# Strassen projection of a fused gMLP block: its operand sums moved from GpSimd to VectorE, with five VectorE operations moved earlier and the last pair's closing piece moved later

## The chip, the cores and the metric

The kernel runs on one core of a Trainium2 chip. The metric is the device time of one execution in microseconds (us). Three runs of the kernel before took 311.89, 312.03 and 312.06 us, so the median is 312.03 us. The profile is of one execution; it records a span of 309.7 us, and some 2.3 us of the device time lie around that span.

The engines are named as in the profile: PE (TensorE), PEld (its weight loads), DVE (VectorE), ACT (ScalarE), POOL (GpSimd), and SP (SyncE, which here only issues DMAs). SPq and DVEq are the engines' sequencers.

## What is computed

```python
h = layernorm(x) * (1 + ca) + sa                      # x: 2048 x 640
x = x + ga * A(h, k, v, shift_k, ssm_k, ssm_D)        # a long convolution
h = layernorm(x) * (1 + cb) + sb
z = gelu(h @ w_in)                                    # 2048 x 1728
z1, z2 = z[:, :864], layernorm(z[:, 864:])
g = w_sp @ z2 + b_sp[:, None]                         # w_sp: 2048 x 2048
out = x + gb * ((z1 * g) @ w_out)                     # w_out: 864 x 640
```

`u = z1 * g` below. The change lies in the last two lines, and in the order of some preparations during the two lines ahead of them.

## The kernel before

The rows are cut into 16 tiles of 128. After the long convolution (to some 147 us of the span) comes the **z stage**: layernorm, modulation, the product with `w_in`, GELU and the second layernorm. All work up to the first pair of the mix stage is recorded as operations with numbers and then written out in the order of a table by hand, `ORDER`; an entry such as `D1047` puts operation 1047 on DVE at that place. Each engine works through its own instructions in the order in which they stand.

**The mix stage** takes the tiles in pairs: pair p is tile p and tile p + 8, with p = 0 to 7. Pair 0 is in the table; pairs 1 to 7 are the loop at the end of the kernel. `w_sp @ z2` is computed for a pair by Strassen's method in Winograd's form, with seven products instead of eight (`product(p, m)`, each of 8 matmuls 128x432). They come in the order 1, 5, 2, 6, 7, 3, 4 and share four PSUM banks: products 2, 3 and 4 accumulate onto a bank that an earlier product has filled.

- The weights' operand sums are `s_sum(p, k)`, DVE, 128x1024, line 987. They are made one pair ahead.
- After product 2 DVE runs `c11` (L1029); after product 6 `partial` (L1034); after product 7 `c22` (L1038, L1039, L1040). Product 4 accumulates onto the bank that L1038 reads, so PE may not start it before L1038 has ended.
- After products 3 and 4 come `last_sum` (L1045, L1046, twice) and `turn_u` (L1051), a transposing DMA on SP that makes `uT`, the transposed u of a tile.

**The projection** `u @ w_out` of a pair is Strassen-Winograd as well (`project_pair`). The 864 features make 7 chunks; six of them form two halves of three chunks, the seventh (96 rows) is added plainly. Its operand sums are

- `V[0..3]` and `V5`, sums of `w_out` (already multiplied by `gb`, L1076), 128x960 each and one of 96x320, made once (L1160, L1234);
- `R[0..3]`, sums of the pair's `uT` chunks, 128x384 each, made for each pair by `u_sums` (L1170).

`project_pair` returns four pieces that the loop places. `begin` and `most` hold most of its matmuls, on four more banks called a, d, b and c_; ACT copies two of them (L1196, L1198), POOL adds rows of x to them (L1199, L1204, L1205, L1206), DVE makes L1203 and L1211. `sums` is L1216, L1217 and an output DMA (L1218). `end` is the piece that reuses bank c_ after L1216 has read it: 4 matmuls (`V[3]`, `V5`), L1223 and an output DMA (L1224).

In the loop before, the iteration of pair p runs products 1, 5, 2, then `end` of pair p - 2, then products 6, 7, 3, 4, then `begin`, `most` and `sums` of pair p - 1, and then `u_sums(p)` on POOL. After the loop the last two tiles, 7 and 15, are projected plainly (`project`, L1139, L1141), with `end` of pair 6 between them.

Of the kernel before, what the change touches and what calls it, by code (L numbers as in the profile page):

```python
# [10 lines left out]
ALU = mybir.AluOpType  # L11
# [65 lines left out]
D859 A865 P886 A881 A883 G909 P853 D1053 D1049 D966 G907 D968 P884 A854 D862 D807 P892 G908 D800 P871 A885 D810 S910  # L77
D803 A887 A872 D912 P890 D863 D876 P888 G911 P878 A913 D873 A891 A915 D914 A889 A879 P916 A893 G970 S1041 P923 D797
P940 D1054 D971 A972 A917 G975 D811 D974 D804 A941 P926 D869 D855 P919 A927 D866 P952 A920 D852 P933 P954 D856 S1040
D870 D1055 D1052 A953 A924 D1058 D918 P937 G973 D1059 S976 D978 G828 P930 A979 A934 D1050 D928 A938 G977 D980 D925 A981  # L80
D829 A955 D942 D877 D833 D921 A931 D831 P958 G894 S1043 P982 P996 P1006 A983 D932 A959 A830 A832 D922 A1007 D935 D939
D943 D1057 D936 D895 P999 P1003 D1056 A1000 P992 D929 A1004 A997 P950 A993 A951 P948 D994 D898 D1005 A897 A896 P946
D1001 P1018 A949 P985 D998 D1062 G960 A947 D1002 D899 D1008 P989 A1019 A986 P956 D961 P1024 P1012 A964 D963 D962 D1009
A990 D987 A965 D991 P1014 D995 D984 A957 D988 A1025 A1013 G1026 A1015 D1051 P944 D1066 P1070 D1027 A945 D1063 A1030
P1020 A1029 S1042 D1064 P1072 A1071 D1028 A1021 D1031 D1065 P1074 D1068 D1067 P1077 D1075 P1081 P1022 A1073 P1076 D1069
D1078 D1082 D1079 P1083 S1080 P1010 P1016 A1017 D1084 A1011 S1085 D1047 A1023 D1061 D1046 D1048 D1060
"""


# [39 lines left out]
def kernel(  # L129
# [20 lines left out]
    nc = tc.nc  # L150
    _, S, D = A_q.shape
# [5 lines left out]
    NFT = (Fh + P - 1) // P  # L157
# [4 lines left out]
    HS = D // NH  # L162
# [47 lines left out]
    with ExitStack() as pctx:  # L210
# [17 lines left out]
        sums = consta.tile([P, NT, 2], F32)  # L228
# [6 lines left out]
        op = plan.op  # L235
# [735 lines left out]
        def load_w(t):  # L971
            wTs[t] = bwork.tile([P, NT, P], BF16, tag="wT", bufs=WB, name="wT")
            nc.sync.dma_start_transpose(wTs[t][:], B_w_sp[t * P:(t + 1) * P, :])  # L973
# [7 lines left out]
        def s_sum(p, k):  # L981
            if p not in Ss:
                Ss[p] = [bwork.tile([P, HT, P], BF16, tag="S%d" % i, bufs=2, name="S%d" % (i + 1)) for i in range(4)]
            S = Ss[p]
            x, y, o = ((a_of(p, 1, 0), a_of(p, 1, 1), ALU.add), (S[0][:], a_of(p, 0, 0), ALU.subtract),
                       (a_of(p, 0, 0), a_of(p, 1, 0), ALU.subtract), (a_of(p, 0, 1), S[1][:], ALU.subtract))[k]
            nc.vector.tensor_tensor(S[k][:], x, y, op=o)  # L987
# [13 lines left out]
        def product(p, m, alloc):  # L1001
            S = Ss.get(p)
            lhs = (a_of(p, 0, 0), a_of(p, 0, 1), S and S[3][:], a_of(p, 1, 1), S and S[0][:], S and S[1][:], S and S[2][:])[m - 1]
            rhs = (lambda s_: zb(s_, 1, 0), lambda s_: zb(HT + s_, 1, 0), lambda s_: zb(HT + s_, 1, 1),
                   lambda s_: T[4][:, s_:s_ + 1, :], lambda s_: T[1][:, s_:s_ + 1, :], lambda s_: T[2][:, s_:s_ + 1, :],
                   lambda s_: zb(s_, 1, 1))[m - 1]
            more = m in (2, 3, 4)
            if not more:
                part[p, BANK[m]] = alloc(BANK[m])
            ps = part[p, BANK[m]]  # L1010
            for s_ in range(HT):
                nc.tensor.matmul(ps[:, :FC], lhsT=lhs[:, s_, :], rhs=rhs(s_), start=(s_ == 0 and not more), stop=(s_ == HT - 1),  # L1012
                                 skip_group_check=more)
# [111 lines left out]
    w_o = T["w_o"]  # L1125
# [22 lines left out]
    fl = fsz[-1]  # L1148
    vbuf = bigp.tile([P, (4 * KT + 1) * HS], BF16, tag="big", bufs=SLOTS["big"], name="V")
    V = [vbuf[:, i * KT * HS:(i + 1) * KT * HS].rearrange("p (k d) -> p k d", d=HS) for i in range(4)]  # L1150
    V5 = vbuf[:, 4 * KT * HS:]
    rbuf = span.tile([P, 2, 4, KT, P], BF16, tag="Z", bufs=SLOTS["Z"], name="R")
    obuf = span.tile([P, 6, HS], F32, tag="Z", bufs=SLOTS["Z"], name="O")
# [4 lines left out]
    def weight_sum(e, k):  # L1158
        x, y = ((wo_b(0, 1), wo_b(0, 0)), (wo_b(1, 1), V[0]), (wo_b(1, 1), wo_b(0, 1)), (wo_b(1, 0), V[1]))[k]
        e.tensor_tensor(V[k], x, y, op=ALU.subtract)  # L1160
# [4 lines left out]
    def u_sums(p):  # L1165
        R = [rbuf[:, p % 2, i] for i in range(4)]
        lo, hi = p, p + HT
        for k, (x, y, o) in enumerate(((u_of(hi, 0), u_of(hi, 1), ALU.add), (R[0], u_of(lo, 0), ALU.subtract),
                                       (u_of(lo, 0), u_of(hi, 0), ALU.subtract), (u_of(lo, 1), R[1], ALU.subtract))):
            nc.gpsimd.tensor_tensor(R[k], x, y, op=o)  # L1170
        return R

    def rows(i):
# [6 lines left out]
    def project_pair(p, R):  # L1180
        lo, hi = p, p + HT
        U = {(i, j): (lambda k, t=t, j=j: uTs[t][:, j * KT + k, :]) for i, t in ((0, lo), (1, hi)) for j in range(2)}
        B = {(i, j): (lambda k, i=i, j=j: w_o[:, i * KT + k, j * HS:(j + 1) * HS]) for i in range(2) for j in range(2)}
        S_ = [lambda k, i=i: R[i][:, k, :] for i in range(4)]
        V_ = [lambda k, i=i: V[i][:, k, :] for i in range(4)]

        def rest(t, j):
            return (lambda k: uTs[t][:fl, NFT - 1, :]), (lambda k: w_o[:fl, NFT - 1, j * HS:(j + 1) * HS]), 1
        ot = [bwork.tile([P, D], BF16, tag="ot", bufs=3, name="ot") for _ in range(2)]
        x_of = lambda i, j: xt[:, (lo, hi)[i], j * HS:(j + 1) * HS]  # L1190
        m1, m5, s, s12, s21, s22 = (rows(i) for i in range(6))
        a, d, b, c_ = (obank() for _ in range(4))

        def begin():
            piece(a, U[0, 0], B[0, 0], KT, True, True)
            nc.scalar.copy(m1, a[:, :HS])  # L1196
            piece(d, S_[0], V_[0], KT, True, True)
            nc.scalar.copy(m5, d[:, :HS])  # L1198
            nc.gpsimd.tensor_tensor(m5, m5, x_of(1, 1), op=ALU.add)  # L1199

        def most():
            piece(b, S_[1], V_[1], KT, True, True)
            nc.vector.tensor_tensor(s, b[:, :HS], m1, op=ALU.add)  # L1203
            nc.gpsimd.tensor_tensor(s22, s, m5, op=ALU.add)  # L1204
            nc.gpsimd.tensor_tensor(s12, s, x_of(0, 1), op=ALU.add)  # L1205
            nc.gpsimd.tensor_tensor(s21, s, x_of(1, 0), op=ALU.add)  # L1206
            piece(c_, S_[2], V_[2], KT, True, False)
            piece(c_, *rest(hi, 1), False, True)
            piece(a, U[0, 1], B[1, 0], KT, False, False)
            piece(a, *rest(lo, 0), False, True)  # L1210
            nc.vector.tensor_tensor(ot[0][:, 0:HS], a[:, :HS], x_of(0, 0), op=ALU.add)  # L1211
            piece(d, S_[3], B[1, 1], KT, False, False)
            piece(d, *rest(lo, 1), False, True)

        def sums():
            nc.vector.tensor_tensor(ot[1][:, HS:D], c_[:, :HS], s22, op=ALU.add)  # L1216
            nc.vector.tensor_tensor(ot[0][:, HS:D], d[:, :HS], s12, op=ALU.add)  # L1217
            nc.sync.dma_start(out_nat[:, lo, :], ot[0][:])  # L1218

        def end():  # L1220
            piece(c_, U[1, 1], V_[3], KT, False, False)
            piece(c_, lambda k: uTs[hi][:fl, NFT - 1, :], lambda k: V5[:fl, :], 1, False, True)
            nc.vector.tensor_tensor(ot[1][:, 0:HS], c_[:, :HS], s21, op=ALU.add)  # L1223
            nc.sync.dma_start(out_nat[:, hi, :], ot[1][:])  # L1224
        return begin, most, sums, end

    load_w(3)
    load_w(3 + HT)
    weight_sum(nc.gpsimd, 2)
    weight_sum(nc.vector, 0)  # L1230
    R = u_sums(0)
    weight_sum(nc.gpsimd, 1)
    weight_sum(nc.gpsimd, 3)
    nc.gpsimd.tensor_tensor(V5[:fl, :], w_o[:fl, NFT - 1, 0:HS], w_o[:fl, NFT - 1, HS:D], op=ALU.subtract)  # L1234
    end = None
    for p in range(1, HT):
        nxt = p + 1 < HT
        product(p, 1, bank)
        keep(p, 1)
        product(p, 5, bank)  # L1240
        keep(p, 5)
        if nxt:
            s_sum(p + 1, 0)
            s_sum(p + 1, 1)
        product(p, 2, bank)
        c11(p)
        if nxt:
            s_sum(p + 1, 2)
        if end:
            end()  # L1250
        product(p, 6, bank)
        partial(p)
        product(p, 7, bank)
        c22(p)
        begin, most, sums, end = project_pair(p - 1, R)
        product(p, 3, bank)
        last_sum(p, "d", 0, 1)
        turn_u(p, 0)
        product(p, 4, bank)
        last_sum(p, "c", 1, 0)  # L1260
        turn_u(p, 1)
        if p + 3 < HT:
            load_w(p + 3)
            load_w(p + 3 + HT)
        begin()
        most()
        if nxt:
            s_sum(p + 1, 3)
        sums()
        if nxt:  # L1270
            R = u_sums(p)
    project(HT - 1)
    end()
    project(NT - 1)
# [30 lines left out]
```

## Time and profile before

| | us |
|---|---|
| device time, median of 3 runs | 312.03 (311.89 to 312.06) |
| span of the profiled execution | 309.7 |
| busy in the span: PE, DVE, POOL, ACT | 295.1, 272.4, 186.2, 164.1 |
| products of pair 0 end, pair 1 of the loop starts on PE | 203.6 |
| last matmul of the program ends | 306.9 |

How to read the rows: a timeline row gives start, duration, engine, line, operation, what it writes and reads, and how many instructions it stands for; in brackets at its end stands how long the engine was idle just before, and what ended that. Durations are from issue to completion, so instructions that follow each other on DVE overlap in the records by 0.05 to 0.1 us, and a row of matmuls includes 0.16 us of the pipeline's tail, during which the next matmul may already run. POOL's spans are rough.

### The profile page before, as it was taken

The numbers are of one execution on the slowest core, as the hardware profiler recorded it, in microseconds if no ns is written. First come the engines' busy times: TensorE is split into PE (matmuls) and PEld (weight loads), VectorE is DVE, ScalarE is ACT, GpSimd is POOL, SyncE is SP. The second block draws the span as 40 slices with busy tenths as digits, with TensorE's granted clock in tenths as the row PEclk, the third lists the DMA queues.
The fourth block names the chain that finished last, engine by engine and source line by source line (L and its number), as shares of the span: only waits on it lengthen the run. The fifth ranks groups of instructions, "written<-read, shape, count | busy, mean of one in ns | idle before, by whom it ended". The sixth has DMA issues, their size and how long they took to land.

```text
span 309.7 us, 6534 instructions
## 1 busy us (share of the span) xinstructions
PE 295.1 (95%) x2485; PEld 195.4 (63%) x2485; DVE 272.4 (88%) x532; ACT 164.1 (53%) x298; POOL 186.2 (60%) x209
## 2 busy tenths in 40 slices
PE   6979999999999999899999999998899999999995
PEld 1357678797889998755554555555455656565554
DVE  7797999999999999998859788999999878888574
ACT  4799699989787864466647799031111111021110
POOL 5724955856869999695705312049658474573922
PEclk9799999999999999999999999999999999999999
DMA  7999999999674949505898800073387593730323
GB/s 176 224 251 200 243 299 199 249 254 207 170 158 115 184 110 273 211 3 108 191 181 180 150 1 1 2 145 51 73 167 150 132 194 73 168 80 21 83 55 110
DMA packets 127954, 45.23 MB, mean 146 GB/s; under 512 B 117071, under 2 KB 127156, under 8 KB 127924
## 3 DMA queue, kind: packets, MB, share of 16 engines
q1 hardware_dynamic: 127770, 44.78, 65.5%
q8 instruction: 19, 0.31, 0.4%
q14 instruction: 11, 0.09, 0.1%
q10 hardware_dynamic: 154, 0.05, 0.1%
HBM read 16.11 MB, written 5.24 MB: 69 GB/s over the span
## 4 chain that ended last, share of the span: by engine, by line
PE 40%; DVE 6%; DMA 4%; SPq 4%; POOL 2%; issue 1%; ACT 0%; DVEq 0%; ACTq 0%
PE ps L1012 20%; PE po L1178 7%; PE pu L244 4%; PE pz L244 4%; DMA Z<-Z 3%; SPq L973 2%; PE pz L1012 2%; PE pu L1012 1%; DVE S L987 1%; PE po L1139 1%; SPq L1073 1%; DMA uT<-u 1%; POOL Z L844 1%; DVE V L1160 1%; POOL xt L697 1%
## 5 line engine op out<-in xcount | busy, mean ns | idle before, releaser
L244 PEld LDWEIGHTS <-Z 128*128 128x128 bf16 x320 | 31.1, 98 | 28.4 <-issue 1.2
L244 PE MATMUL pu<-X,M 128*128 128x128 bf16 (+1 forms) x480 | 45.9, 237 | 0.4 <-DVE Tf L461 0.3
L244 PEld LDWEIGHTS <-M 128*128 128x128 bf16 x480 | 37.1, 98 | 5.3 <-issue 0.6
L475 POOL TENSOR_TENSOR W<-Tf 128x256 bf16<-128x256 f32 x43 | 31.3, 745 | 12.7 <-DVE Tf L461 5.0
L1012 PEld LDWEIGHTS <-S 128*128 128x128 bf16 x256 | 25.0, 98 | 21.2
L244 PE MATMUL pu<-big,Z 128*128 128x432 bf16 x160 | 33.6, 346 | 0.5 <-ACT M L919 0.4
L244 PE MATMUL pz<-big,Z 128*128 128x432 bf16 x160 | 32.6, 346 | 0.1
L1196 ACT COPY O<-po 128x320 f32<-128x320 f32 x7 | 3.0, 427 | 55.9 <-PE po L1178 55.9
L247 ACT CAST X<-s 128x1024 bf16<-128x1024 f32 x30 | 30.7, 1024 | 3.5 <-PE s L244 3.4
L461 DVE TENSOR_TENSOR Tf<-pu,KH 128x1024 f32<-128x1024 f32 x25 | 30.0, 1214 | 1.4 <-PE pu L244 1.0
L1012 PEld LDWEIGHTS <-wT 128*128 128x128 bf16 x192 | 18.7, 98 | 17.6 <-issue 2.0
L244 PEld LDWEIGHTS <-G 128*128 128x128 bf16 x330 | 25.0, 98 | 3.3 <-issue 0.6
L247 ACT CAST KH<-pu 128x512 bf16<-128x512 f32 x40 | 23.5, 598 | 6.0 <-PE pu L244 6.0
L247 ACT CAST Z<-pz 128x512 bf16<-128x512 f32 x34 | 19.9, 599 | 8.2 <-PE pz L244 8.1
L1199 POOL TENSOR_TENSOR O<-O,xt 128x320 f32<-128x320 f32 x7 | 6.3, 906 | 28.0 <-ACT O L1198 28.0
L1012 PE MATMUL ps<-T,S 128*128 128x432 bf16 x112 | 22.7, 346 | 0.0
L1012 PE MATMUL ps<-X,wT 128*128 128x432 bf16 x112 | 22.7, 346 | 0.0
L244 PE MATMUL sm<-big,dg 128*128 128x512 bf16 (+1 forms) x80 | 21.3, 395 | 0.7 <-ACT dg L535 0.7
L1012 PE MATMUL ps<-X,S 128*128 128x432 bf16 x112 | 21.6, 346 | 0.0
L244 PEld LDWEIGHTS <-X 128*128 128x128 bf16 x288 | 18.2, 97 | 5.2 <-issue 1.4
L244 PE MATMUL s<-F1bd,X 128*128 128x256 bf16 x128 | 19.2, 273 | 0.3 <-ACT X L247 0.3
L925 DVE BATCH_NORM_STATS2 stz<-X 128x6 f32<-128x432 bf16 x32 | 17.8, 589 | 1.6 <-ACT X L919 1.6
(208 smaller groups left out, 679.9 us busy)
## 6 DMA issues: line engine op xcount, KB each, us to landing
wm<-in_w_mod_dram SPq DMA_DIRECT2D x6, 800.0 KB, 6.1
xt<-in_A_q_dram SPq DMA_DIRECT2D x4, 640.0 KB, 5.2
out_dram<-ot SPq DMA_DIRECT2D x15, 160.0 KB, 2.2
big<-in_B_w_in_dram SPq DMA_DIRECT2D x2, 1080.0 KB, 10.7
X<-in_A_ssm_k_dram SPq DMA_DIRECT2D x4, 512.0 KB, 7.0
kv_scr<-big SPq DMA_DIRECT2D x4, 512.0 KB, 3.2
X<-kv_scr SPq DMA_DIRECT2D x4, 512.0 KB, 4.5
w_o<-in_B_w_out_dram SPq DMA_DIRECT2D x6, 160.0 KB, 3.4
```

Source lines behind the costliest of these rows:

```text
L244: nc.tensor.matmul(o, lhsT=w, rhs=x, start=start, stop=stop)
L247: (e.copy if e is nc.scalar else e.tensor_copy)(dst, src)
L461: e.tensor_tensor(T_[:], (tl[pu] if src is None else tl[src])[:, :, :, None, :].to_broadcast(shape), tl[KH][:, :, None, :, :].to_broadcast ...
L475: e.tensor_tensor(tl[W][:, :, o, :], T_[:, :, 0, o, :], T_[:, :, 1, 1 - o, :], op=ALU.add if o else ALU.subtract)
L697: op("GD" if u < NU - 1 else "D", "res", lambda e: e.tensor_tensor(sl, sl, gl, op=ALU.add), r=[("gh", (u, g))], w=[("xt", (u, n)) for n in ...
L844: e.tensor_scalar(dst, xt[:, n, :], rstd2[:, n:n + 1], nmr2[:, n:n + 1], op0=ALU.mult, op1=ALU.add)
L925: op("D", "stz", lambda e, i=i, n=n, fc=fc: e.bn_stats(out=stz[:, n, fc, :], in_=tl[z2][:, i, fc * FC:(fc + 1) * FC]), r=[(z2, (i, fc))], ...
L973: nc.sync.dma_start_transpose(wTs[t][:], B_w_sp[t * P:(t + 1) * P, :])
L987: nc.vector.tensor_tensor(S[k][:], x, y, op=o)
L1012: nc.tensor.matmul(ps[:, :FC], lhsT=lhs[:, s_, :], rhs=rhs(s_), start=(s_ == 0 and not more), stop=(s_ == HT - 1), skip_group_check=more)
L1178: nc.tensor.matmul(ps[:, :HS], lhsT=w(k), rhs=x(k), start=start and k == 0, stop=stop and k == n - 1, skip_group_check=True)
L1199: nc.gpsimd.tensor_tensor(m5, m5, x_of(1, 1), op=ALU.add)
```

## The change

1. `u_sums` runs on DVE instead of POOL, and stands one iteration later: `R = u_sums(p - 1)` after product 5 of pair p and the first two `s_sum`s, ahead of product 2 and `c11`.
2. The five sums `V[0..3]` and `V5`, of which POOL made four, are all made by DVE, in one row ahead of the loop.
3. In the table, five DVE operations that stood at its end are moved up into the z stage: 1046, 1047, 1048 and 1051, four of the seven multiplications of `w_out` by `gb` (L1076), and 1061, the sum `s_sum(1, 3)` (L987).
4. In the last iteration (p = 7) `end` of pair 5 stands after product 4, instead of between products 2 and 6.

```diff
-            nc.gpsimd.tensor_tensor(R[k], x, y, op=o)
+            nc.vector.tensor_tensor(R[k], x, y, op=o)
...
-    weight_sum(nc.gpsimd, 2)
-    weight_sum(nc.vector, 0)
-    R = u_sums(0)
-    weight_sum(nc.gpsimd, 1)
-    weight_sum(nc.gpsimd, 3)
-    nc.gpsimd.tensor_tensor(V5[:fl, :], w_o[:fl, NFT - 1, 0:HS], w_o[:fl, NFT - 1, HS:D], op=ALU.subtract)
+    for k in (0, 2, 1, 3):
+        weight_sum(nc.vector, k)
+    nc.vector.tensor_tensor(V5[:fl, :], w_o[:fl, NFT - 1, 0:HS], w_o[:fl, NFT - 1, HS:D], op=ALU.subtract)
...
             s_sum(p + 1, 1)
+        R = u_sums(p - 1)
         product(p, 2, bank)
...
-        if end:
+        if end and nxt:
             end()
...
-        begin, most, sums, end = project_pair(p - 1, R)
...
+        if not nxt:
+            end()
+        begin, most, sums, end = project_pair(p - 1, R)
         begin()
         most()
...
         sums()
-        if nxt:
-            R = u_sums(p)
```

Of the table, the entries `D1047 D1046 D1048` now follow `D1059`; `D1061 D1051` follow `D929`.

**DVE, between pair 0 and the c22 of pair 1.** `w_o` is `w_out`, `S_...` the weights' sums, `u_...` the rows of u, `T_...`, `s_...` and `c_...` intermediate sums, `ps` and `po` PSUM banks. Before:

```order
L1046 TENSOR_TENSOR u_2796<-c,G_81 128x432
L1076 TENSOR_TENSOR w_o<-w_o,gb_bf 128x640
L987 TENSOR_TENSOR S_3083<-wT,S_3081 128x1024
L1076 TENSOR_TENSOR w_o<-w_o,gb_bf 128x640 x2
L987 TENSOR_TENSOR S_3082<-wT 128x1024
L1160 TENSOR_TENSOR V<-w_o 128x960
L987 TENSOR_TENSOR S_3464<-wT 128x1024
L987 TENSOR_TENSOR S_3465<-S_3464,wT 128x1024
L1029 SCALAR_TENSOR_TENSOR u_2797<-ps,bcol,M_80 128x432
```

and the same stretch now:

```order
L1046 TENSOR_TENSOR u_2796<-c,G_81 128x432
L987 TENSOR_TENSOR S_3082<-wT 128x1024
L1160 TENSOR_TENSOR V<-w_o 128x960 x2
L1160 TENSOR_TENSOR V<-w_o,V 128x960 x2
L1231 TENSOR_TENSOR V<-w_o 96x320
L987 TENSOR_TENSOR S_3460<-wT 128x1024
L987 TENSOR_TENSOR S_3461<-S_3460,wT 128x1024
L1170 TENSOR_TENSOR R<-uT 128x384
L1170 TENSOR_TENSOR R<-R,uT 128x384
L1170 TENSOR_TENSOR R<-uT 128x384
L1170 TENSOR_TENSOR R<-uT,R 128x384
L1029 SCALAR_TENSOR_TENSOR u_2797<-ps,bcol,M_80 128x432
```

Four operations have left this place for the z stage; three V sums, V5 and the four R sums of pair 0 have come in from POOL.

**DVE, where the moved operations now stand in the z stage** (`Z` is the modulated input, `X_...` z2, `mvz` and `stz` its statistics):

```order
L929 BN_AGGR mvz<-stz 128x2
L987 TENSOR_TENSOR S_3083<-wT,S_3081 128x1024
L1076 TENSOR_TENSOR w_o<-w_o,gb_bf 128x640
L925 BN_STATS stz<-X_3135 128x6
L942 TENSOR_SCALAR X_2857<-X_2857,mvz,rstdz 128x864
```

The sum and one multiplication stand between a finished statistic and a row (L925) that waits for ACT; the other three multiplications stand in the same manner ahead of an L896 that waits for a transposing DMA.

**DVE, last pair and end of the program.** Before:

```order
L1217 TENSOR_TENSOR ot<-po,O 128x320
L1029 SCALAR_TENSOR_TENSOR u_2797<-ps,bcol,G_81 128x432
L1223 TENSOR_TENSOR ot<-po,O 128x320
L1034 TENSOR_TENSOR s_4320<-ps,m_4283 128x432
L1038 TENSOR_TENSOR c_4331<-ps,s_4320 128x432
```

and, later in the same list, now:

```order
L1046 TENSOR_TENSOR u_2797<-c,G_81 128x432
L1045 SCALAR_TENSOR_TENSOR c<-ps,bcol,s_4314 128x432
L1046 TENSOR_TENSOR u_2798<-c,G_81 128x432
L1223 TENSOR_TENSOR ot<-po,O 128x320
L1203 TENSOR_TENSOR O<-po,O 128x320
L1211 TENSOR_TENSOR ot<-po,xt 128x320
```

L1223 of pair 5, which stood behind `c11` of pair 7, now stands behind the pair's last L1046. On PE its four matmuls stand behind product 4, and on SP its output DMA behind the last two `turn_u`.

More of the change, by code (lines that the diff above doesn't have):

```diff
@@ L79 @@
 P940 D1054 D971 A972 A917 G975 D811 D974 D804 A941 P926 D869 D855 P919 A927 D866 P952 A920 D852 P933 P954 D856 S1040
[L80 to L86, printed above, removed]
+D870 D1055 D1052 A953 A924 D1058 D918 P937 G973 D1059 D1047 D1046 D1048 S976 D978 G828 P930 A979 A934 D1050 D928 A938
+G977 D980 D925 A981 D829 A955 D942 D877 D833 D921 A931 D831 P958 G894 S1043 P982 P996 P1006 A983 D932 A959 A830 A832
+D922 A1007 D935 D939 D943 D1057 D936 D895 P999 P1003 D1056 A1000 P992 D929 D1061 D1051 A1004 A997 P950 A993 A951 P948
+D994 D898 D1005 A897 A896 P946 D1001 P1018 A949 P985 D998 D1062 G960 A947 D1002 D899 D1008 P989 A1019 A986 P956 D961
+P1024 P1012 A964 D963 D962 D1009 A990 D987 A965 D991 P1014 D995 D984 A957 D988 A1025 A1013 G1026 A1015 P944 D1066 P1070
+D1027 A945 D1063 A1030 P1020 A1029 S1042 D1064 P1072 A1071 D1028 A1021 D1031 D1065 P1074 D1068 D1067 P1077 D1075 P1081
+P1022 A1073 P1076 D1069 D1078 D1082 D1079 P1083 S1080 P1010 P1016 A1017 D1084 A1011 S1085 A1023 D1060
 """
```

## The prediction

> **What bounds the kernel now.** I read the page's busy shares first, then the waits of PE from 160 us on, then the busy time of each engine pair by pair in the mix stage, then the timeline around each wait of PE. The page and the waits (who waited for whom: total, times, longest):
>
> ```profile
> PE 295.1 (95%) x2485; PEld 195.4 (63%) x2485; DVE 272.4 (88%) x532; ACT 164.1 (53%) x298; POOL 186.2 (60%) x209
> ```
> ```profile
> PE ps L1012 <- DVE c L1038: 1.5, 2, 0.8
> PE po L1178 <- DVE ot L1216: 1.1, 1, 1.1
> PE po L1139 <- DMA uT<-u: 0.6, 1, 0.6
> ```
>
> PE is the bound, and in the last half of the program it stands still four times: three times for DVE, once for a transposing DMA at the end. Where those three lie is seen from the busy times of pairs 1, 2 and 6 (length of the stretch; then PE, PEld, DVE, ACT, POOL; clock, DMA share, GB/s), each stretch cut from the pair's first product to the next pair's:
>
> ```profile
> 203.60:217.63 14.03, 13.25 (x79) 7.52 (x77) 13.75 (x15) 3.35 (x7) 12.24 (x8) 1.00 0.53 100
> 217.63:233.35 15.72, 13.95 (x83) 7.89 (x81) 14.82 (x23) 1.99 (x4) 9.64 (x10) 1.00 0.61 124
> 274.26:287.89 13.63, 13.63 (x84) 7.91 (x82) 12.06 (x19) 1.99 (x4) 8.51 (x9) 1.00 0.24 58
> ```
>
> A settled pair takes 13.63 us with PE full, at full clock. Pairs 1 and 2 are longer, and in them DVE is busy nearly throughout. The timeline tells why DVE is late there:
>
> ```profile
> 205.23 2.33 POOL L1160 TENSOR_TENSOR V<-w_o 128x960 bf16<-128x960 bf16 x1 [14.78 <-PE ps L1012]
> 205.62 2.46 DVE L1160 TENSOR_TENSOR V<-w_o 128x960 bf16<-128x960 bf16 x1
> 212.75 4.32 POOL L1160 TENSOR_TENSOR V<-w_o,V 128x960 bf16<-128x960 bf16 x2
> 213.31 1.62 PE L1012 MATMUL ps<-T,wT 128*128 128x432 bf16 x8 [0.78 <-DVE c L1038]
> 213.36 1.85 DVE L1039 TENSOR_TENSOR c<-c,m 128x432 f32<-128x432 f32 x1
> 215.25 2.29 DVE L1040 TENSOR_TENSOR u<-c,G 128x432 bf16<-128x432 f32 x1
> 223.23 0.70 PE L1178 MATMUL po<-V,uT 128*128 128x320 bf16 x4 [1.05 <-DVE ot L1216]
> 229.03 1.62 PE L1012 MATMUL ps<-T,wT 128*128 128x432 bf16 x8 [0.72 <-DVE c L1038]
> 282.30 0.61 DVE L1038 TENSOR_TENSOR c<-ps,s 128x432 f32<-128x432 f32 x1 [0.53 <-PE ps L1012]
> 283.01 0.61 DVE L1039 TENSOR_TENSOR c<-c,m 128x432 f32<-128x432 f32 x1
> 283.65 0.61 DVE L1040 TENSOR_TENSOR u<-c,G 128x432 bf16<-128x432 f32 x1
> ```
>
> L1039 and L1040 take 0.61 us in pair 6, and 1.85 and 2.29 us in pair 1, beside POOL's V sums. So DVE operations that read two SBUF tensors come to a stand while POOL does the same. The one V sum on DVE shows it exactly: it starts at 205.62, POOL's ends at 207.56, and DVE's at 208.08, 0.52 later.
>
> **Part by part.** *The sums that leave POOL* (parts 1 and 2 of the change) take away this cause. What it costs now is read from the lengths of the pairs; pair 1 has no `end` piece, whose price stands in pair 7:
>
> ```profile
> 292.27 0.71 PE L1178 MATMUL po<-V,uT 128*128 128x320 bf16 x4
> 292.81 1.62 PE L1012 MATMUL ps<-T,S 128*128 128x432 bf16 x8
> ```
>
> Pair 2 is 15.72 - 13.63 = 2.09 us too long. `end` takes 292.81 - 292.27 = 0.54 us of PE; pair 1 does without it, so its length should be 13.09, and it is 0.94 too long. Together 3.03 us. The three idle times 0.78, 1.05 and 0.72 make 2.55; the difference is three times the 0.16 us of the pipeline's tail, which the row of `end` shows too (0.71 long, the next one 0.54 later).
>
> What do the sums cost on DVE? No R, and no V without POOL beside it, is in the trace. The nearest rows are other two-input bf16 operations of DVE while POOL was quiet:
>
> ```profile
> 163.76 0.64 DVE L987 TENSOR_TENSOR S<-wT 128x1024 bf16<-128x1024 bf16 x1
> 172.24 0.48 DVE L1076 TENSOR_TENSOR w_o<-w_o,gb_bf 128x640 bf16<-128x640 bf16 x1
> 188.53 1.05 DVE L997 TENSOR_TENSOR X<-X,X 128x1728 bf16<-128x1728 bf16 x1
> ```
>
> A V (960 elements) lies between 0.48 and 0.64; I take 0.61, as it is close to 1024. The 1728-element row works on four pieces of 432 and costs no more for it, so the three pieces of 320 in V add nothing. An R (384 elements) is at most 0.48; carried on from 1024 and 640 it is 0.37, from 1728 and 1024 it is 0.27. I take 0.33, four of them 1.3, with 1.1 to 1.9 as bounds; V5 at most that, 0.3.
>
> Is there room on DVE in pair 1? The last row of pair 0 ends at 203.29, and L1038 has to end by the time when product 4 may start:
>
> ```profile
> 202.68 0.61 DVE L1046 TENSOR_TENSOR u<-c,G 128x432 bf16<-128x432 f32 x1
> 207.52 1.32 POOL L1170 TENSOR_TENSOR R<-uT 128x384 bf16<-128x384 bf16 x1
> 209.44 3.08 PE L1012 MATMUL ps<-X,S 128*128 128x432 bf16 x16
> ```
>
> Products 7 and 3 end their issue at 209.44 + 3.08 - 0.16 = 212.36. From 203.29 DVE now has: one S 0.64, four V 2.44, V5 0.3, two S 1.28, four R 1.3, `c11` 0.66, an S 0.64, L1034 0.6, L1038 0.61: 8.47 us, so 211.8, 0.6 us ahead of need. In it R begins at 207.95, and `uT` of pair 0 is there by then, since POOL's R began at 207.52. With the upper prices (V 0.64, R 0.48) it is 212.5, and 0.1 us of the hole would stay. Pair 1 then leaves DVE where the settled pairs have it, and the two holes of pair 2 have no cause left. I count the whole 3.0.
>
> *The wait that this adds.* R on DVE waits for the pair's `uT`, and `c11`, an S sum, L1223, L1034 and L1038 are queued behind it; PE waits for the last. Pair 3 has the transposes that landed latest:
>
> ```profile
> 250.13 0.69 DVE L987 TENSOR_TENSOR S<-S,wT 128x1024 bf16<-128x1024 bf16 x1
> 250.55 1.03 POOL L1170 TENSOR_TENSOR R<-uT 128x384 bf16<-128x384 bf16 x1 [1.01 <-DMA uT<-u]
> 255.04 0.61 DVE L1038 TENSOR_TENSOR c<-ps,s 128x432 f32<-128x432 f32 x1 [0.79 <-PE ps L1012]
> ```
>
> They landed at 250.5, DVE is through with the S sum at 250.8: no wait. R ends at 252.1, and 0.66 + 0.64 + 0.48 + 0.6 later, at 254.5, DVE is ready for L1038, which waits for PE until 255.04 in any case. And L1038 may be later still by the time of product 3, 1.46 (half of the 2.92 above), less its own 0.61. So a settled pair hides R with 0.5 us to spare, 1.3 until PE waits. Cost 0.
>
> *The five moved operations* (part 3) are counted above as gone from pair 0's end. Where they go, DVE waits:
>
> ```profile
> 171.91 0.41 DVE L896 TENSOR_SCALAR Z<-Z,cb_col,sb_col 128x512 bf16<-128x512 bf16 x1 [1.90 <-DMA Z<-Z]
> 180.46 0.61 DVE L925 BATCH_NORM_STATS2 stz<-X 128x6 f32<-128x432 bf16 x1 [1.13 <-ACT X L919]
> ```
>
> Three multiplications, 3 x 0.48 = 1.4, stand in the gap of 1.90; the sum and the fourth, 0.64 + 0.48 = 1.12, in that of 1.13, with the overlap of the records to spare. Their inputs are there, since other L1076 and other sums of the same weights have run by then. Cost 0; if a cover were gone, a few tenths, and only if PE then waits.
>
> *The end* (part 4). Pair 7, with the rows that set the last steps:
>
> ```profile
> 293.08 0.49 DVE L1223 TENSOR_TENSOR ot<-po,O 128x320 bf16<-128x320 f32 x1
> 299.06 1.39 PE L1178 MATMUL po<-V,R 128*128 128x320 bf16 x9
> 299.92 0.61 DVE L1046 TENSOR_TENSOR u<-c,G 128x432 bf16<-128x432 f32 x1
> 299.26 2.57 SPq L1051 DMA_TRANSPOSE uT<-u  x2
> 301.38 0.30 PE L1178 MATMUL po<-w_o,uT 96*128 96x320 bf16 x1
> 302.30 2.08 PE L1139 MATMUL po<-w_o,uT 128*128 128x320 bf16 x14 [0.61 <-DMA uT<-u]
> ```
>
> Times here are those of before. With the four matmuls of `end` behind product 4, products 6, 7, 3 and 4, the last L1046 and the transposes come 0.54 earlier: the transpose is issued at 298.72 and lands at 301.7, not 302.25. PE's own work is the same in sum, so all that can be won is its idle time, 0.6 by the row, at most 0.55 by the transposes. But L1223 now runs behind the last L1046, which ends at 299.99, and so ends at 300.4. The third group of V x R matmuls writes the bank that L1223 reads; nine take 1.39 - 0.16, so it would start at 299.06 + 6 x 0.137 = 299.88, and has to wait until some 300.45. The row at 301.38 then ends its issue at 301.52 + 0.57 = 302.09, and PE comes to tile 7 there instead of at 302.30. I take 0.2; bounds 0 and 0.55. On SP the output DMA of L1224 goes out behind both transposes, at about 301.3. Its buffer is wanted again by L1141 of tile 7 at about 303.2:
>
> ```profile
> out_dram<-ot SPq DMA_DIRECT2D x15, 160.0 KB, 2.2
> ```
>
> It lands at 303.5, so L1141 may be 0.3 late, and nothing waits for that for the next microsecond.
>
> **The sum.** Against the profiled execution: 309.7 - 3.0 - 0.2 = 306.5. The median of the runs lies 2.3 above that span, and I keep the 2.3: **308.8 us**, 1.0% less. A difference of 0.2%, 0.6 us, is about what a measurement of this kernel tells from none.
>
> **The rivals.** *VectorE becomes the bound* (the other side). DVE is busy 12.06 us of a settled pair's 13.63. Four R at 0.33 add 1.3. But two S sums of pair 6 ran beside POOL's R:
>
> ```profile
> 277.39 1.28 DVE L987 TENSOR_TENSOR S<-S,wT 128x1024 bf16<-128x1024 bf16 x1
> 279.42 1.44 DVE L987 TENSOR_TENSOR S<-wT 128x1024 bf16<-128x1024 bf16 x1
> ```
>
> They fall back to 0.64, which gives the same 1.4 again. That speaks against. For it speaks that R has no row on DVE. Without any relief 1.57 us are free, so R binds from 0.39 each on, with the relief from 0.75; at POOL's 1.03 four R are 4.1, DVE needs 12.06 - 1.4 + 4.1 = 14.8, and six pairs (2 to 7) lose 1.15 each, 6.9 us, against 3.2 won: 315.7. It is slower than before from R = 0.88 on. The Trainium skill, Perfetto Trace Analysis, section Optimizing Scalar/DVE Operations, speaks against this change in the same sense: work is to be taken off VectorE where it is saturated, if need be to GpSimd, though it adds that between those two this may not help, since they share a port. The rule's first half would give this rival, its second half my forecast; the V rows above agree with the second. Chance 0.04.
>
> *V is slow by itself.* The only V on DVE took 2.46 us. If that is its own price and not POOL's doing, four take 9.8 instead of 2.44, L1038 of pair 1 ends at 219.2, PE waits 6.8 us there instead of 0.94, and 2.3 are won elsewhere: 315.6. Against it: 1728 elements took 1.05. It is slower than before from about 1.6 us per V on. The Trainium skill, SBUF — State Buffer, section Who interferes with whom, says that an operation of VectorE with two SBUF inputs and one of GpSimd that reads SBUF exclude each other for a whole instruction, so that the later one stands still; by that V is the 0.52 us left after POOL's end, and the sum is the one I made. Chance 0.02.
>
> *A hole stays.* Pair 1 has only 0.6 us to spare. If `uT` of pair 0 lands late or the prices are at their upper ends and more, the 0.94 of pair 1 stays and nothing is won at the end: 309.9. If what delays pair 2 is not pair 1's delay carried on, 2.09 stay: 310.9. Speaking against it: DVE's 0.5 to 0.8 us of waiting for PE in every settled pair. Chance 0.10.
>
> *Nothing changes.* The holes are filled but other ones open, for instance a settled pair's R behind transposes that land over 2 us later than any here, so that six pairs give 0.5 back each: 312.0. Chance 0.04.
>
> **How the numbers follow.** The forecast has 0.80: 308.8, its own range 308.4 to 309.2 from the end's 0 to 0.55, the 0.1 of pair 1 and the runs' 0.15. To hold 8 in 10 with sizes that no row shows, the range takes in the first case of the hole that stays, and below it some relief elsewhere on DVE: 308.3 to 310.2. Outside are the 310.9, the nothing, and the slower cases, with some 0.05 below. Faster: 0.80 + 0.10 = 0.90; same 0.04; slower 0.06.
>
> **What would show it.** Right: the PE waits for L1038 and L1216 gone, pairs 1 and 2 at 13.1 and 13.63 us; POOL without V and R; V at about 0.6 and R at about 0.33 on DVE; L1039 and L1040 of pair 1 at 0.61; the gaps at 171.9 and 180.5 nearly filled, and PE full there; PE waiting for L1223 for half a microsecond behind product 4 of pair 7, and the `uT` wait gone. Wrong: a PE wait for L1038 that comes again pair by pair (R too dear or `uT` late), V above 1.5, or a PE wait in the z stage.

## The result, and the profile after

| | before | after |
|---|---|---|
| median, us | 312.04 (311.40 to 312.22, 6 runs) | 308.88 (308.08 to 309.95, 6 runs) |
| span of the profiled execution, us | 309.7 | 306.6 |
| ratio after / before, 95% interval | | 0.9899 (0.9879 to 0.9919) |

The kernel is 1.0% faster, 3.2 us by the medians. The profiled execution took 308.4 us in all.

The page's first line on the engines, of after:

```profile
PE 292.7 (95%) x2478; PEld 194.8 (64%) x2485; DVE 271.9 (89%) x564; ACT 164.4 (54%) x298; POOL 147.2 (48%) x177
```

POOL has lost 39 us of work and 32 instructions, DVE has gained 32 instructions and no busy time: 272.4 us before, 271.9 now. What DVE took over it got back from its own operations, which no longer stand still. The busy shares alone would show a kernel in which nothing has happened to PE or DVE.

The waits of PE from 160 us on, of after (who waited for whom: total, times, longest):

```profile
PE pz L244 <- ACT X L919: 0.5, 1, 0.5
PE po L1178 <- DVE ot L1223: 0.4, 1, 0.4
PE po L1139 <- DMA uT<-u: 0.2, 1, 0.2
```

The three waits for L1038 and L1216 are gone. There is a new one for L1223, which the prediction had announced, and the wait for the last transposes is shorter but not gone. The first row lies in the z stage; the section on the prediction comes back to it.

Pairs 1, 2, 6 and 7 of after, the last up to tile 7 (length; then PE, PEld, DVE, ACT, POOL; clock, DMA share, GB/s):

```profile
203.34:216.43 13.09, 13.09 (x79) 7.53 (x78) 12.09 (x24) 3.35 (x7) 1.27 (x2) 1.00 0.62 124
216.43:230.06 13.63, 13.63 (x84) 7.91 (x81) 11.90 (x23) 1.99 (x4) 3.76 (x5) 1.00 0.66 136
270.96:284.59 13.63, 13.63 (x83) 7.92 (x81) 11.89 (x23) 1.99 (x4) 3.76 (x5) 1.00 0.24 58
284.59:299.19 14.60, 13.96 (x83) 7.81 (x81) 10.50 (x21) 1.99 (x4) 4.73 (x6) 1.00 0.30 55
```

Pairs 1 and 2 are as long as PE's own work in them. They were 14.03 and 15.72, so 0.94 and 2.09 us have come from there.

The span's difference of 3.1 us can be placed whole. From the first product of pair 1 to that of pair 7 it was 287.89 - 203.60 = 84.29, and is 284.59 - 203.34 = 81.25: 3.04 less. Pair 1 begins 0.26 earlier. From pair 7's first product to the start of the last L1141 it was 306.90 - 287.89 = 19.01 and is 303.79 - 284.59 = 19.20: 0.19 given back. The 0.26 is no part of the change: the start of pair 1, 203.34 here, lies anywhere between 203.2 and 205.2 in the traces of the experiments, with the old table and with the new one.

DVE in pair 1 of after, in order, from the timeline (dots stand for rows left out):

```profile
203.55 1.22 DVE L1160 TENSOR_TENSOR V<-w_o 128x960 bf16<-128x960 bf16 x2
204.69 1.34 DVE L1160 TENSOR_TENSOR V<-w_o,V 128x960 bf16<-128x960 bf16 x2
205.95 0.31 DVE L1231 TENSOR_TENSOR V<-w_o 96x320 bf16<-96x320 bf16 x1
...
207.51 0.35 DVE L1170 TENSOR_TENSOR R<-uT 128x384 bf16<-128x384 bf16 x1
...
210.84 0.61 DVE L1038 TENSOR_TENSOR c<-ps,s 128x432 f32<-128x432 f32 x1 [0.36 <-PE ps L1012]
211.56 0.61 DVE L1039 TENSOR_TENSOR c<-c,m 128x432 f32<-128x432 f32 x1
212.20 0.61 DVE L1040 TENSOR_TENSOR u<-c,G 128x432 bf16<-128x432 f32 x1
```

All four V sums are through in 2.4 us (203.55 to 205.95), where a single one took 2.46 us beside POOL. L1039 and L1040, 1.85 and 2.29 us before, are at 0.61. And L1038 now waits 0.36 us for PE; before, PE waited 0.78 us for it.

The end of after, from the timeline:

```profile
295.35 2.63 SPq L1051 DMA_TRANSPOSE uT<-u  x2
...
296.61 0.48 DVE L1223 TENSOR_TENSOR ot<-po,O 128x320 bf16<-128x320 f32 x1
297.14 0.57 PE L1178 MATMUL po<-V,R 128*128 128x320 bf16 x3 [0.40 <-DVE ot L1223]
298.03 0.65 SPq L1224 DMA_DIRECT2D out_dram<-ot  x1
299.19 2.08 PE L1139 MATMUL po<-w_o,uT 128*128 128x320 bf16 x14 [0.25 <-DMA uT<-u]
...
300.52 0.49 DVE L1141 TENSOR_TENSOR ot<-po,xt 128x320 bf16<-128x320 f32 x1 [0.58 <-DMA out_dram<-ot]
```

Everything that the prediction listed is there: PE idle behind L1223, the output DMA behind both transposes, and L1141 late for it. What it did not have is that the transpose of tile 7, the first of the two and the one PE waits for, lands 3.8 us after its issue (issued at 295.35, the last of its 16 completion signals at 299.14), where before's took 3.0 (299.26 to 302.25).

### The profile page after: what moved, and what is told of

Its sections match the earlier page's. It is cut to its first block, busy times and chain, and to the rows that moved or that the text cites. A ratio compares the mean times of both kernels' runs of the same rounds, so it can differ in the third digit from the quotient of the medians.

```text
span 306.6 us, 6495 instructions
## 1 busy us (share of the span) xinstructions
PE 292.7 (95%) x2478; PEld 194.8 (64%) x2485; DVE 271.9 (89%) x564; ACT 164.4 (54%) x298; POOL 147.2 (48%) x177
## 5 line engine op out<-in xcount | busy, mean ns | idle before, releaser
L1012 PEld LDWEIGHTS <-wT 128*128 128x128 bf16 x192 | 18.8, 98 | 15.8
L244 PE MATMUL sm<-big,dg 128*128 128x512 bf16 (+3 forms) x73 | 19.6, 380 | 1.9 <-DVE big L552 0.8
L461 DVE TENSOR_TENSOR T<-pu,KH 128x1024 bf16<-128x1024 f32 x15 | 18.2, 1216 | 0.3 <-PE pu L244 0.3
```

The costliest lines, as they stand in the source:

```text
L244: nc.tensor.matmul(o, lhsT=w, rhs=x, start=start, stop=stop)
L461: e.tensor_tensor(T_[:], (tl[pu] if src is None else tl[src])[:, :, :, None, :].to_broadcast(shape), tl[KH][:, :, None, :, :].to_broadcast ...
```

## The experiments

Each kernel ran beside runs of the kernel before on the same chip; times are medians, ratios are to the kernel before with the 95% interval. Three chips were used, one for each group below.

### Which part carries the gain

**The table alone (part 3).** The kernel before with only the table's lines changed; the first of them shows it:

```diff
-D870 D1055 D1052 A953 A924 D1058 D918 P937 G973 D1059 S976 D978 G828 P930 A979 A934 D1050 D928 A938 G977 D980 D925 A981
+D870 D1055 D1052 A953 A924 D1058 D918 P937 G973 D1059 D1047 D1046 D1048 S976 D978 G828 P930 A979 A934 D1050 D928 A938
```

> The kernel before with the table of after (five DVE operations moved into the z stage) and nothing else. Theory (POOL's V and R sums hold off DVE's operations with two SBUF inputs): DVE comes to pair 1 about 1.8 us earlier, so the hole of 0.94 us in pair 1 closes, but L1039 and L1040 still stand beside V sums on POOL and the 2.09 us of pair 2 stay: about 311.1 us. Rival (DVE merely has too much work ahead of pair 1, and the table is what relieves it): all three holes close, about 309.0.

Measured: 310.08 us, ratio 0.9942 (0.9919 to 0.9966). Pairs 1 and 2 in its trace:

```profile
203.19:216.28 13.09, 13.09 (x79) 7.53 (x77) 11.90 (x12) 3.35 (x7) 12.57 (x9) 1.00 0.55 107
216.28:231.32 15.04, 13.95 (x83) 7.90 (x81) 14.17 (x22) 1.99 (x4) 8.97 (x9) 1.00 0.67 129
```

The hole of pair 1 is closed, as expected, and pair 2 has shrunk as well, from 15.72 to 15.04. That is 0.94 + 0.68 = 1.6 us, against 1.9 by the medians: more than the theory, less than the rival, and both sizes were wrong. The V sums on POOL hold DVE off as before (L1039 and L1040 of pair 1 took 1.77 and 2.29 us), but DVE enters pair 1 earlier, so less of the delay is left in pair 2.

**The old table with everything else (parts 1, 2 and 4).** The kernel after with the table of before.

> The kernel after with the table of before: V and R on DVE, the five operations back at the end of pair 0. Theory: DVE has 1.8 us more ahead of pair 1's L1038; in the profile of after it waited 0.36 there and PE had some 0.65 to spare, so about 0.8 us of PE wait in pair 1 and none later: about 309.7. Rival (the table is what relieves DVE): the three holes are back, 311.5 or more.

Measured: 310.15 us, ratio 0.9942 (0.9922 to 0.9962). PE waits for L1038 once, 0.8 us, in pair 1, which is 14.03 us long as before the change; pair 2 is 13.63. So the hole of pair 1 stays whole when only the sums move: DVE's row ahead of L1038 is then too long with the V sums in it, and the four moved operations are what makes room. Table alone 1.6 us, sums alone 2.1, both 3.0: the two parts overlap by 0.7, and neither closes both holes.

**V on DVE, R on POOL.** The kernel after with R as before:

```diff
-            nc.vector.tensor_tensor(R[k], x, y, op=o)
+            nc.gpsimd.tensor_tensor(R[k], x, y, op=o)
...
+    R = u_sums(0)
...
-        R = u_sums(p - 1)
...
+        if nxt:
+            R = u_sums(p)
```

> The kernel after with the R sums back on POOL at their old place (behind the sums of the pair before); V on DVE, table and end as in after. Theory: V alone made the holes, since the settled pairs of before bear R on POOL without a PE wait; the S sums beside R take up to 1.44 us again, L1170 on POOL 0.9 to 1.36, and the time is that of after, 308.9 (up to 309.2). Rival (R on POOL makes a hole of its own where DVE is late): 0.5 to 1 us more, 309.4 to 309.9.

Measured: 308.67 us, ratio 0.9888 (0.9868 to 0.9908), no different from after. Pairs 1 and 2 are 13.08 and 13.64. Two groups of its trace, R and one form of the S sums (count | busy, mean ns | idle before):

```profile
L987 DVE TENSOR_TENSOR S<-S,wT 128x1024 bf16<-128x1024 bf16 x6 | 7.1, 1186 | 0.2
L1170 POOL TENSOR_TENSOR R<-uT 128x384 bf16<-128x384 bf16 x14 | 16.0, 1144 | 18.0 <-DMA uT<-u 18.0
```

R on POOL makes S sums twice as long, but in a stretch in which DVE has the time. The move of R is worth nothing here; V and the table carry the gain. The Trainium skill, Perfetto Trace Analysis, section Optimizing Scalar/DVE Operations, adds to its advice to relieve a saturated VectorE that a shift between it and GpSimd might not help; for R that holds in both directions, 308.67 with it on GpSimd and 308.88 on VectorE.

**R on DVE, V on POOL.** The kernel after with the V sums as before:

```diff
-    for k in (0, 2, 1, 3):
-        weight_sum(nc.vector, k)
...
+    weight_sum(nc.gpsimd, 2)
+    weight_sum(nc.vector, 0)
+    weight_sum(nc.gpsimd, 1)
+    weight_sum(nc.gpsimd, 3)
```

> The kernel after with the V sums back on POOL (three of four and V5); R on DVE at its new place, table and end as in after. Theory: POOL's V sums now start earlier (w_o is ready in the z stage) and stand beside the S and R sums of pair 1 from about 204 to 210 us, each DVE sum waiting for a V of 2.2 us: L1038 of pair 1 ends near 213.4 instead of 211.5, a PE wait of about 1.3 us in pair 1, none in pair 2: about 310.2. Rival (R's move to DVE is what gained): 308.9.

Measured: 312.45 us, ratio 1.0010 (0.9982 to 1.0039): in the median the whole gain is gone. Its timeline in pair 1:

```profile
205.46 2.47 POOL L1160 TENSOR_TENSOR V<-w_o 128x960 bf16<-128x960 bf16 x1 [13.53 <-PE pz L244]
205.99 2.49 DVE L987 TENSOR_TENSOR S<-wT 128x1024 bf16<-128x1024 bf16 x1
207.89 4.85 POOL L1160 TENSOR_TENSOR V<-w_o,V 128x960 bf16<-128x960 bf16 x2
208.51 2.37 DVE L987 TENSOR_TENSOR S<-S,wT 128x1024 bf16<-128x1024 bf16 x1
210.81 2.15 DVE L1170 TENSOR_TENSOR R<-uT 128x384 bf16<-128x384 bf16 x1
...
216.82 2.42 PE L1012 MATMUL ps<-T,wT 128*128 128x432 bf16 x8 [2.69 <-DVE c L1038]
```

With no R between them on POOL, its three V sums follow each other, and each of three DVE sums stands behind one of them: two S sums at 2.4 to 2.5 us and an R at 2.15 that takes 0.36 alone. A second R took 0.83 beside POOL's V5. The hole is 2.7 us, where 1.3 was expected: two such meetings had been counted, and there are three and a short one. The mechanism holds; only its count was off.

The hole is not all that this run lost. Pair 1 is 17.61 us long in this trace, 4.52 more than in after, and the hole with the pipeline's tail is 2.85 of it. The rest begins in PE's last row above, in which eight matmuls take 2.42 us instead of 1.62. From there to the end of the pair (216.82 to 222.82) the granted clock is 0.72 on average: it is 0.50 for 3.4 us from 217.49 on. Whether the hole brings this on is not tested. The profiled execution is also the slowest of twelve (310.42 to 314.38 us), so the share of the clock in the median of 312.45 is not known.

### What on GpSimd holds VectorE off, and how much room VectorE has

**Fills instead of the V sums on POOL.** The kernel before with:

```diff
-    weight_sum(nc.gpsimd, 2)
+    for _ in range(2):
+        nc.gpsimd.memset(V[2], 0.0)
```

and the same for V 1 and 3 and V5.

> The kernel before, with GpSimd's three V sums and V5 replaced by fills (six fills of V with zeros, two for each sum, so that GpSimd stays about as long at work there, and one for V5): GpSimd writes, but reads nothing. The V sum on VectorE and all R sums stay as they were; three of the V sums are left out, so the output lacks them. Theory (a VectorE operation with two SBUF inputs is held off by a GpSimd operation that reads SBUF, for its whole length): L1039 and L1040 of pair 1 take 0.61 us, the V sum on VectorE 0.65, the waits of PE for L1038 and L1216 go, and the time is about 309.0 (3.0 less than before). Rival (any GpSimd work beside it slows VectorE, or what delays pair 1 is V being ready late): L1039 and L1040 stay at about 2 us, waits of 0.7 to 1.1 stay, 311.5 to 312.5.

Measured: 309.15 us, ratio 0.9919 (0.9892 to 0.9946). Its timeline:

```profile
203.62 1.85 POOL L1230 MEMSET V<- 128x960 bf16 x2 [13.38 <-PE pz L244]
205.41 0.65 DVE L1160 TENSOR_TENSOR V<-w_o 128x960 bf16<-128x960 bf16 x1
210.89 1.85 POOL L1234 MEMSET V<- 128x960 bf16 x2
211.61 0.61 DVE L1039 TENSOR_TENSOR c<-c,m 128x432 f32<-128x432 f32 x1
212.25 0.61 DVE L1040 TENSOR_TENSOR u<-c,G 128x432 bf16<-128x432 f32 x1
```

POOL writes beside L1039 and L1040, and they take 0.61 us. Pairs 1 and 2 are 13.08 and 13.63: the whole 3 us is won with the old table and R on POOL. So POOL being busy is not what costs, and neither is its writing.

**Copies instead.** The same with `nc.gpsimd.tensor_copy(V[2], wo_b(0, 1))` and so on.

> The same with copies in place of the fills: GpSimd reads one SBUF tensor of 128x960 and writes it to V, twice for each of its three sums, and once for V5. Again three V sums are left out. Theory (reading SBUF at all is what counts): as before the change, L1039 and L1040 of pair 1 at 1.3 to 2.3 us, the V sum on VectorE behind the first copy, PE waits for L1038 and L1216 of 0.5 to 1.0, and 311 to 312. Rival (only two-input GpSimd operations hold VectorE off, as the prediction put it): 0.61 us, no waits, about 309.0 as with fills.

Measured: 309.73 us, ratio 0.9926 (0.9902 to 0.9949). Its timeline:

```profile
205.73 2.67 POOL L1230 COPY V<-w_o 128x960 bf16<-128x960 bf16 x2 [14.78 <-PE ps L1012]
206.12 1.44 DVE L1160 TENSOR_TENSOR V<-w_o 128x960 bf16<-128x960 bf16 x1
213.16 2.68 POOL L1234 COPY V<-w_o 128x960 bf16<-128x960 bf16 x2
213.72 1.27 DVE L1040 TENSOR_TENSOR u<-c,G 128x432 bf16<-128x432 f32 x1
215.89 0.97 PE L1178 MATMUL po<-V,R 128*128 128x320 bf16 x6 [0.59 <-POOL V L1234]
```

A copy, with one input, does hold DVE off: the V sum takes 1.44 us, ends 0.5 us after the first of the two copies, and L1040 doubles. In this the theory is right and the prediction's wording ("while POOL does the same", that is, reads two tensors) too narrow. The time, though, fell between the two: one copy is 1.34 us long, not 2.3, DVE loses less, and of the waits for L1038 and L1216 only 0.2 us, in pair 2 (13.86 long), is left. PE waits instead for V itself, which two copies in a row deliver late; pair 1 is 13.84 us long, 0.75 too long, which is this 0.59 and the pipeline's tail of 0.16. The Trainium skill, SBUF — State Buffer, section Who interferes with whom, draws the line in the same place: VectorE with two SBUF inputs contends with a GpSimd instruction that reads SBUF, not with one that only writes it. The two runs agree: 0.61 us beside fills, 1.27 beside a copy.

**R three times over.** The kernel after with:

```diff
-        R = u_sums(p - 1)
+        for _ in range(3):
+            R = u_sums(p - 1)
```

> The kernel after with each pair's four R sums made three times over on VectorE (the same result is written again). An R takes 0.36 us there, so eight more add 2.9 us of VectorE to each pair. Theory (VectorE has room for 1.7 us more in a settled pair, 13.63 - 11.9, and binds beyond): settled pairs go from 13.63 to about 14.8 us with VectorE full, six of them 7 us, less the 1 us or so of lead: 314 to 316, slower than before. Rival (records overlap and VectorE has far more room, or product 2 and what follows hide the whole): settled pairs stay at 13.63 to 13.9 and the time at 309 to 310.5.

Measured: 319.42 us, ratio 1.0244 (1.0205 to 1.0284). The waits of PE, and pairs 2 and 6:

```profile
PE ps L1012 <- DVE c L1038: 9.5, 6, 1.8
PE po L1178 <- DVE ot L1223: 1.0, 1, 1.0
```
```profile
218.61:233.93 15.32, 13.80 (x84) 7.91 (x82) 14.49 (x31) 1.99 (x4) 3.60 (x4) 1.00 0.72 120
280.30:295.67 15.37, 13.79 (x84) 7.91 (x81) 14.53 (x31) 1.99 (x4) 3.60 (x4) 1.00 0.21 52
```

It is slower than before, as the theory said, but by 10.5 us against after where 5 to 7 were expected. Twelve R sums follow each other in 3.59 us (238.44 to 242.03 in pair 3), so eight more add 2.4 us to each pair, not the 2.9 that their durations make: the records overlap. The theory took the free room from the busy time, 13.63 - 11.9 = 1.7. The five pairs 2 to 6 (from 218.61 to 295.67, 77.06 us) are 15.41 long on average, 1.78 longer, so the room was 2.4 - 1.8 = 0.6 us. DVE is at its limit with 14.5 busy of 15.4: some 0.9 us of each pair are lost in short waits inside DVE's row (L1217 behind POOL's L1205, for instance). The prediction's other estimate, 1.3 us until PE waits, read from the chain to L1038 in one pair, is nearer, but also twice too high.

### The end

After again and three placements of pair 5's `end`, all on one chip. What tells them apart is not the total, which moves by a microsecond between runs, but the stretch from pair 7's first product to the start of the last L1141.

> The kernel after once more, for the runs beside it. From pair 7's first product to the last L1141 it took 19.20 us in its profile, against 19.01 before: 308.9.

After, repeated: 309.27 us, ratio 0.9893 (0.9863 to 0.9923), so the result stands. Its end, though, is 304.96 - 285.42 = 19.54 us long: tile 7's uT landed 4.1 us after its issue (296.18 to 300.31), and PE waited 0.6 us for it, besides 0.4 for L1223.

**`end` at its old place (without part 4).**

```diff
-        if end and nxt:
+        if end:
...
-        if not nxt:
-            end()
```

> The kernel after with part 4 undone: end of pair 5 stands between products 2 and 6 of pair 7 as before. Theory (the move of end costs 0.2 us: L1223 holds a bank for 0.4 and the output DMA that follows makes the transposes land late): PE waits 0.6 for uT and not for L1223, the transposes land 3.0 after issue, 19.0 us from pair 7's first product to the last L1141, 0.2 less than after: 308.7. Rival (the move brings the 0.2 that was forecast): 19.4 us and 309.1.

Measured: 308.23 us, ratio 0.9881 (0.9858 to 0.9904); the stretch is 303.81 - 284.95 = 18.86 us, tile 7's uT landed 2.9 us after its issue, and PE waited 0.5 us for it. Part 4 is no gain: without it the kernel is at least as fast.

**`end` one step earlier, behind product 3.**

```diff
         turn_u(p, 0)
+        if not nxt:
+            end()
         product(p, 4, bank)
```

> The kernel after with end of pair 5 one product earlier in the last iteration: behind product 3, the last_sum and the turn_u of tile 7, so that L1223 runs ahead of the second L1045. Theory: L1223 is through before the third V x R group, so its wait is gone, and uT of tile 7 is issued as early as in after; but the output DMA of L1224 goes out while it is under way, so it lands about 3.8 after issue and PE waits for it: 19.15 us from pair 7's first product, about the time of after. Rival (the output DMA does not matter): it lands 3.0 after issue, 18.65 us, 0.55 less than after.

Measured: 307.64 us, ratio 0.9864 (0.9836 to 0.9892). The stretch is 303.05 - 284.73 = 18.32 us, 0.9 less than after. In the timeline:

```profile
295.33 0.48 DVE L1223 TENSOR_TENSOR ot<-po,O 128x320 bf16<-128x320 f32 x1
295.49 1.23 SPq L1051 DMA_TRANSPOSE uT<-u  x1
296.77 0.57 SPq L1224 DMA_DIRECT2D out_dram<-ot  x1
297.45 1.57 SPq L1051 DMA_TRANSPOSE uT<-u  x1
298.45 2.08 PE L1139 MATMUL po<-w_o,uT 128*128 128x320 bf16 x14
```

This is the rival's side, and more than it asked. L1223 is through at 295.81, before PE needs its bank, so that wait is gone. Tile 7's uT landed 2.9 us after its issue (298.40). The first L1139 group starts with no idle time of PE ahead of it, although the output DMA now stands between the two transposes.

**The same, with the output DMA last.** L1224 of pair 5 is issued behind pair 6's L1218, and tile 7's output has a buffer of its own.

> The same, and the output DMA of pair 5's second tile is issued behind that of pair 6's first (tile 7's output is built in a free S buffer, so that it needs not wait for it). Theory: with nothing behind the transposes, uT of tile 7 lands 3.0 after issue and PE waits neither for L1223 nor for it: 18.65 us from pair 7's first product to the last L1141, 0.55 less than after, 308.3. Rival (the transposes land late for another reason): 19.15 us.

Measured: 308.06 us, ratio 0.9869 (0.9846 to 0.9893); the stretch is 303.08 - 284.77 = 18.31 us. The place of the output DMA makes no difference, then, once PE does not wait for L1223.

**Behind product 3, with R on POOL** (the edits of that run and of the one with V alone together; it ran with the fills, the copies and the threefold R).

> The kernel after with two edits that were looked at apart: the R sums back on GpSimd and at their old place, and the end piece of pair 5 behind product 3 of the last iteration. Theory (R's place and engine are worth nothing, the end piece behind product 3 leaves PE no wait at the end and is worth 0.5 to 0.9): 307.6 to 308.2, from pair 7's first product to the last L1141 18.3 us. Rival (on GpSimd, R slows VectorE where the end piece has used up its room): 308.5 or more, with a wait for L1038 or L1223.

Measured: 307.93 us, ratio 0.9873 (0.9832 to 0.9915); the stretch is 303.41 - 285.01 = 18.40 us, with no wait of PE from pair 1 on. R's engine is worth nothing here either. The totals of after and of the three kernels with `end` behind product 3 have overlapping intervals; the stretch, 18.3 to 18.4 in all three against 18.8 to 19.5 in the traces with `end` behind product 4, does tell them apart.

## Why the prediction was right

The time (308.8 against 308.88) and the span (306.5 against 306.6) came out as forecast, and the steps but one with them. That they agree to 0.1 us is partly luck: the end missed its forecast by 0.39 us, and pair 1 happened to begin 0.26 earlier. The 2.3 us between the span and the median came out again, though only 1.8 lie around the span of the execution that was profiled (308.4 - 306.6).

- **The cause.** That POOL's sums hold DVE's two-input operations off is shown from three sides: with the sums on DVE the holes are gone; with V back on POOL a hole of 2.7 us is there; with POOL filling instead of adding it is not.
- **The 3.03 us.** Worked out from the lengths of the pairs, measured 3.04. Taking the holes' length from the pairs and not from the idle times in brackets (2.55) was what made this exact.
- **The prices on DVE.** V 0.65 for the forecast 0.61, R 0.36 for 0.33, V5 0.31 for 0.3; in a row the four V take 2.40 us and four R 1.20, where the sum had 2.44 and 1.3. The 0.52 us that was left of V after POOL's sum is 0.13 short of V's own 0.65; the run with V on POOL shows the same 0.13 (0.55 left of an S sum's 0.68, 0.22 of an R's 0.36). These are the two groups of after, in which the means stand:

```profile
L1160 DVE TENSOR_TENSOR V<-w_o 128x960 bf16<-128x960 bf16 x2 | 1.2, 654 | 0.0
L1170 DVE TENSOR_TENSOR R<-uT 128x384 bf16<-128x384 bf16 x14 | 5.1, 364 | 0.0
```

- **The room in pair 1.** Forecast 0.6 us until PE waits, measured 1.0: DVE was ready for L1038 0.36 us before product 7 was done, and L1038 then ended at 211.45, 0.65 before product 4 began at 212.10. The run with the old table shows that this is still thin: without part 3, with 1.8 us more work on DVE ahead of L1038, PE waits 0.8 us there.
- **A settled pair hides R.** Forecast 0.5 to spare and 1.3 until PE waits. L1038 waits 0.78 us for PE in pairs 2, 3 and 5 to 7 and 0.70 in pair 4, where R of pair 3 again starts (247.66) just when the slowest transposes land (247.64). The 0.5 holds; the 1.3 does not, as the threefold R puts the room that lasts from pair to pair at 0.6.
- **The moved operations cost nothing.** After's rows at the two gaps of the z stage:

```profile
169.28 1.28 DVE L1076 TENSOR_TENSOR w_o<-w_o,gb_bf 128x640 bf16<-128x640 bf16 x3
171.64 0.41 DVE L896 TENSOR_SCALAR Z<-Z,cb_col,sb_col 128x512 bf16<-128x512 bf16 x1 [1.08 <-DMA Z<-Z]
180.20 0.61 DVE L925 BATCH_NORM_STATS2 stz<-X 128x6 f32<-128x432 bf16 x1 [0.18 <-ACT X L919]
```

The second gap went from 1.13 to 0.18, nearly filled, the first from 1.90 to 1.08. PE's wait of 0.5 us for ACT in the z stage, which the prediction named as a sign against it, is not theirs. Before has one too, 0.4 us, a fifth wait from 160 us on that the prediction's four leave out; the kernel with copies has the old table and shows 0.6 and 0.4 there, and the kernel with `end` behind product 3 has the new table and shows 0.2.

- **The end: the step that failed.** Forecast 0.2 won, measured 0.19 lost, and 0.53 lost in the repeat. The wait for L1223 was sized well (0.57 with the pipeline's tail, measured 0.40 + 0.16), and the transposes were issued 0.6 us earlier (10.76 us after the pair's first product against 11.37). What failed is "lands at 301.7", the 2.98 us of before carried over. The traces with `end` behind product 4 (the threefold R left out, where PE waits 1.0 us for L1223):

| kernel | tile 7's uT, issue to landing, us | stretch, us |
|---|---|---|
| R on DVE, V on POOL | 2.9 | 18.78 |
| V on DVE, R on POOL | 3.0 | 18.78 |
| the old table | 3.7 | 19.12 |
| after | 3.8 | 19.20 |
| after, repeated | 4.1 | 19.54 |

In the first two the stretch is 0.23 shorter than before's 19.01, the forecast to a few hundredths; in the others the late landing eats it up. The output DMA behind the transposes does not explain this: it stands there in all five. The trace's DMA queues point elsewhere. In the three late traces one packet of 8 KB runs on the queue that the profile calls *instruction* while the transpose is under way; this is its row in after (packets, MB, share of the DMA engines' time from 293 to 305 us), where it starts at 297.99 and takes 0.56 us:

```profile
q14 instruction: 1, 0.01, 0.3%
```

Of tile 7's 16 completion signals the last one or two then come 0.8 to 1.25 us after the others. In the two early traces, and in before, no such packet runs in that time. That this packet is the cause is not shown: with `end` at its old place and behind product 3, with R and V on DVE, it runs as well, and the transpose still lands 2.9 us after its issue.

Of the rivals, *nothing changes* and *a hole stays* did not come about, though the old table shows that the second lay close. *VectorE becomes the bound* is a real mechanism, with 0.6 us more to go before it starts: R would have had to cost (1.2 + 0.6) / 4 = 0.45 us each in a row, between the 0.39 and the 0.75 that the prediction took from the busy times. *V is slow by itself* is refuted by 0.65.

## What to carry to other kernels

Before moving work between GpSimd and VectorE, look at which VectorE rows stretch while GpSimd reads SBUF, and whether a wait of the bounding engine hangs on them: V's four sums, with the table, were worth 3 us and R's 28 nothing, because the delays by R fell where VectorE had time. Size a hole by the length of its stretch against an undisturbed one. Free room is less than idle time: VectorE had 0.6 us where its idle time gave 1.7 and one chain 1.3, and it was at its limit with 94% busy. And a landing read in one kernel need not hold in the next: it was the one term that missed, with 3.8 and 4.1 us in the kernel after for the 3.0 of before.

## What the runs showed of the hardware that was not expected

- GpSimd's fills of SBUF left VectorE's two-input sums at 0.61 us, and its plain copies, with one input, stretched them to 1.27 and 1.44 us.
- Where both engines have two-input sums in a row, they take turns: in the kernel with V back on POOL three VectorE sums in a row took 2.49, 2.37 and 2.15 us, ending 0.55, 0.54 and 0.22 us after a GpSimd sum, although they take 0.68, 0.69 and 0.36 us alone.
- The transposing DMA of tile 7, in the same place of the program, landed 2.9 to 4.1 us after its issue in five traces. It was late only where an 8 KB packet of the instruction queue ran beside it, though not each time one did.
- In the kernel with V back on POOL the granted clock fell to 0.50 for 3.4 us just after PE had stood still for 2.7 us; one trace shows it.
